# A list scheduler that reckons each GpSimd step of a 32x32 inverse longer: delta attention and two feed-forward stages on one core

## The chip, the core and the metric

The kernel runs on one core of a Trainium2 chip. The metric is the device time of one execution in microseconds; three runs of the kernel before were taken, and one execution was recorded by the hardware profiler. Engines: PE is TensorE (matrix products; PEld its weight loads), DVE is VectorE, ACT is ScalarE, POOL is GpSimd, SP is the queue that issues the DMAs.

## What is computed

Inputs are float32 (and are turned to float32 where they come as float64). Three stages follow each other:

```python
# attention: B=4, H=8, S=768, D=48, for each of 32 heads
k_n = k / (norm(k) + 1e-6)
for t in range(S):
    y[t] = q[t] @ state
    v_old = state.T @ k_n[t]
    state = state + beta[t] * outer(k_n[t], v[t] - v_old)
# first feed-forward, 3072 tokens, 384 -> 1024 -> 384
h = x @ w_in;  solu = h * softmax(h)
x = layernorm(solu) * g_ln @ w_out
# second feed-forward, 384 -> 2048 -> 384
out = relu(x @ w_in2) ** 2 @ w_out2
```

## The kernel before

**The work.** The recurrence is done in chunks of 64 tokens. Inside a chunk the sequential update is a triangular system, so each chunk needs the inverse of a unit lower triangular 64x64 matrix; it is built from inverses of 32x32 blocks. The 24 tiles (t = 0 to 23, each two chunks of four pairs of heads) are put in six groups of four (G0, `group`). For a tile, `e_tile` or its parts load q and k, form the products on PE (banks are read by ACT, which writes g, and DVE or POOL, which mask m), and store g in DRAM (gscr). When the four tiles of a group are there, `gammas` makes the factors from the norms and `inversion` (L835) inverts all 128 blocks of the group at once, one block to a partition: 30 columns, each a product (L910) and a sum (L927), columns from the tenth on in two parts. Then one product with gamma (L952) ends it. The result `it` is stored in DRAM (tscr); ACT copies it transposed to `ia` (L969), which is stored too (uscr). For each tile `load_tb` (L985) reads the blocks back as tbd and t2, `prep1` (L1062), `prep2` (L1078, needs t2) and `z` (L1105) apply the inverse on PE, and `a_mm` and `o_mm` run the recurrence. ACT copies the results: ys, tbd, zs (L1119).

The first group (g = 0) is inverted on DVE; the other five are inverted on GpSimd, one after the other. Inside an inverse the planner puts a small memset (L940) on GpSimd after every stretch of steps whose price passes 0.75 us. GpSimd also scales v by the norms (`load_kv`, L1042), does some masks and squares at the start, and makes the low halves `wgl` of the eight pieces of the first output weight (`load_w1o`, through `split`, L420). The weights come as 64-bit words: ACT (L458), DVE (L466 to L502) and ACT again (L539) decode them and scale them by g_ln, and ACT casts the high half wgh (L415).

The first feed-forward runs behind the attention, tile by tile (`moe1_front`: transposes L1204, products L1215, softmax and norm on DVE and ACT; `moe1_back`: transposes L1317, zh and zl), and its output product `moe1_out` (L1337, needs wgh and wgl) for each two tiles. The second feed-forward (L1480, L1524) starts when the attention's buffers are free. Products in float32 are split in a high and a low half and done as three matmuls.

**What sets the order.** The program is not written in the order in which it runs. Every operation is given to the class `Plan` (L116) with its engine, a price in us, the keys it reads and writes, and a priority (its due time). `Plan.order` (L159) runs a list scheduler forward over all operations: whenever an engine is free, it takes from the operations whose inputs are there the one with the smallest key. Between dependent operations it adds 0.1 us on GpSimd and ScalarE, 0.13 us on DVE, and 0.2 us between engines. For DMAs it reckons an issue time, a rate and a tail. Then it runs a backward pass, takes the ends of that as the new keys, and repeats this 12 times; the order of the round with the shortest reckoned span is what is emitted, as one in-order queue for each engine and one for the DMAs on SP. So a price affects nothing but the order. The price of one step on GpSimd is `c_pool` (L271), with n the elements of a partition:

```python
def c_pool(n, full=True):
    return 0.148 + n * (2.104e-3 if full else 1.667e-3)
```

In `inversion` every step goes through `one` (L864), which calls the local function `cost`; a product and the last step pass full=False. The mask `lower` (1.3 us) and the memsets (0.1 us) have prices of their own, and the counter `run`, which places the memsets, calls `c_pool` itself.

Of the kernel before, what the change touches and what calls it, by code (L numbers as in the profile page):

```python
# [262 lines left out]
def c_dve(n, fast=False):  # L263
    return 0.07 + n / (1920.0 if fast else 960.0)
# [6 lines left out]
def c_pool(n, full=True):  # L271

    return 0.148 + n * (2.104e-3 if full else 1.667e-3)
# [3 lines left out]
def tile_delta_moe_moe(  # L277
# [14 lines left out]
    v, act, pool, pe = nc.vector, nc.scalar, nc.gpsimd, nc.tensor  # L292
# [541 lines left out]

    def inversion(g, en, prio):  # L835

        eng, cost = (v, lambda n, full=True: c_dve(n) + 0.09) if en == "dve" else (pool, c_pool)
        gm = gm_[g % 2]
        it, itmp = it_[g % 2], junk[:, 512:] if g == 1 else itmp_
        kgm, kic, kia = ("A", "gm", g % 2), ("A", "itc", g % 2), ("A", "ia")  # L840
# [5 lines left out]
        n = 2 * (G0[g + 1] - G0[g])  # L846
# [54 lines left out]
        for j in range(1, HB - 1):  # L901
            nr = HB - 1 - j
            for q, (c0, c1) in enumerate(((0, min(j, s1)), (s1, j))):
                w_ = c1 - c0
                if w_ <= 0:
# [13 lines left out]
                    full=False,  # L919
# [35 lines left out]
            full=False,  # L955
# [197 lines left out]
    def o_mm(t):  # L1153
        first, last = t % NCH == 0, t % NCH == NCH - 1

        def mm():
            for i in range(2):
                for p in range(NP):
                    for h in range(2):
                        s = rows[h]  # L1160
                        if not last:
                            pe.matmul(ksp[heads[h], i, p], zs_[i][s, p, C:112], R[s, i, p], start=True, stop=True)
                        pe.matmul(  # L1163
                            xp[rows[1 - h], i, p],
                            zs_[i][s, p, 0:C],
                            R[s, i, p],
                            start=first and i == 0 and p == 0,
                            stop=True,
                            skip_group_check=True,
                        )  # L1170

        return mm, [("A", "zs", 0), ("A", "zs", 1), ("A", "r")], [("A", "a"), ("A", "o")]
# [393 lines left out]
    for t in range(T1):  # L1566
        wr = e_tile(t, -70 + t)
        norms(t, -62)
    gammas(0, -61)
    inversion(0, "dve", -55)  # L1570
    first_inv.append(plan.writer["A", "it", 0, 0])
    for t in range(T1, T2):
# [4 lines left out]

    gate.append(wr)
    inversion(1, "pool", PR["inv1"])
    load_w1i(0, 6, PR["w1i"])  # L1580
    for t in range(T2, LA):
# [16 lines left out]
    for t in range(NT + 3):  # L1598
        if t < NT:
            for g in range(2, NG):  # L1600
                if t == max(1, G0[g] - 5):
                    gammas(g, t + PR["inv"])
                    inversion(g, "pool", t + PR["inv"])
# [7 lines left out]
            parts, cost = [], 0.3  # L1611
# [23 lines left out]
            parts, cost = [o_mm(t)], 1.25  # L1635
# [113 lines left out]
```

## Time and profile before

| what | value |
|---|---|
| median of 3 runs | 900.76 us (897.88 to 901.03) |
| the profiled execution, own time | 896.73 us |
| its span, first to last instruction | 895.0 us |
| mean granted TensorE clock | 0.96 of full |
| busy: PE, PEld, DVE, ACT, POOL | 804.2, 748.0, 494.7, 449.6, 311.7 us |
| POOL idle from | 432 us on |

The page's first part gives busy times, its second the span in 40 slices, its fourth the chain of work that ended last, followed back from the end. The busy time of PE is modelled from pipelined matmuls. An idle time of an engine is put down to what released it; a group or a timeline row shows it in brackets ahead of the arrow. Times of the trace count from the start of the span.

### The profile page before, as it was taken

To read this page: it belongs to the slowest core of one execution; us is meant where nothing else is said; L and a number is where in the kernel's file an instruction comes from. 1 tells how busy PE (TensorE), PEld (TensorE's weight loads), DVE (VectorE), ACT (ScalarE), POOL (GpSimd) and SP (SyncE) were. 2 spreads that over 40 slices of the span, in tenths; PEclk is the share of its full clock that TensorE was granted. 3 is DMA by queue.
4 is the path that set the end of the run, shared out by engine and by line. 5 is a ranking of instruction groups with operands and counts; after the bars stand their busy time and mean duration, and the time that the engine had idled before them with its cause. 6 is when DMAs were issued, how large, how long until landed. Compare 5 with 4: busy or idle time off the path is not lost.

```text
span 895.0 us, 24146 instructions
## 1 busy us (share of the span) xinstructions
PE 804.2 (90%) x9904; PEld 748.0 (84%) x9904; DVE 494.7 (55%) x990; ACT 449.6 (50%) x996; POOL 311.7 (35%) x751
## 2 busy tenths in 40 slices
PE   5425759999978989999999999999999999999997
PEld 4324637888867878878889999999999999999997
DVE  5999765634974895775756444343334333343332
ACT  2315568675765675756666444343434333343333
POOL 5469989847978978920000000000000000000000
PEclk9975878999998999999999999999999999999999
DMA  9947866577687686466244311010101001010101
GB/s 243 275 119 175 251 160 172 138 158 187 176 254 190 198 204 188 145 178 182 88 130 127 112 48 53 1 54 1 53 1 38 17 1 53 1 27 1 27 1 27
DMA packets 139726, 99.71 MB, mean 111 GB/s; under 512 B 95072, under 2 KB 120672, under 8 KB 139616
## 3 DMA queue, kind: packets, MB, share of 16 engines
q1 hardware_dynamic: 139616, 98.18, 40.3%
q8 instruction: 77, 1.26, 0.6%
q14 instruction: 33, 0.27, 0.1%
HBM read 71.41 MB, written 26.74 MB: 110 GB/s over the span
## 4 chain that ended last, share of the span: by engine, by line
PE 63%; POOL 12%; DVE 7%; DMA 6%; ACT 5%; issue 3%; SPq 3%; ACTq 0%; POOLq 0%; DVEq 0%
PE acc L1524 22%; PE h L1480 22%; PE p_x L1337 7%; POOL it L927 6%; PE p_h L1215 5%; POOL junk L910 3%; SPq L300 3%; DMA raw<-in_w2i_dram 2%; POOL itmp L910 2%; PE p_tr L1317 2%; PE p_a L1132 1%; DMA m<-in_ktok_dram 1%; PE p_u L1105 1%; PE p_o L1163 1%; DVE zl L420 1%
## 5 line engine op out<-in xcount | busy, mean ns | idle before, releaser
L1501 DVE TENSOR_TENSOR xt<-xt 128x384 f32<-128x384 f32 x128 | 71.5, 558 | 167.3 <-ACT xt L1493 167.1
L1493 ACT ACTIVATE xt<-h 128x384 f32<-128x384 f32 x128 | 63.0, 492 | 167.1 <-PE h L1480 167.0
L1480 PE MATMUL h<-x1l,w2h 128*128 128x384 f32 x384 | 128.7, 335 | 0.0
L1480 PE MATMUL h<-x1h,w2h 128*128 128x384 f32 x384 | 128.6, 335 | 0.0
L1480 PE MATMUL h<-x1h,w2l 128*128 128x384 f32 x384 | 128.5, 335 | 0.0
L927 POOL TENSOR_TENSOR it<-it,itmp 128x72 f32<-128x72 f32 (+37 forms) x204 | 89.4, 454 | 4.6
L1524 PE MATMUL acc<-woh,xh 128*128 128x384 f32 x258 | 87.7, 340 | 0.7 <-ACT ot L1546 0.7
L1337 PE MATMUL p_x<-zh,wgh 128*128 128x256 f32 x288 | 86.2, 299 | 1.9 <-ACT xo L1351 1.8
L1524 PE MATMUL acc<-wol,xh 128*128 128x384 f32 x258 | 87.4, 339 | 0.0
L1524 PE MATMUL acc<-woh,xl 128*128 128x384 f32 x258 | 87.1, 338 | 0.0
L910 POOL TENSOR_TENSOR itmp<-it 128x72 f32<-128x72 f32 (+37 forms) x204 | 85.9, 436 | 2.2
L1337 PE MATMUL p_x<-zl,wgh 128*128 128x256 f32 x288 | 82.1, 285 | 0.0
L1337 PE MATMUL p_x<-zh,wgl 128*128 128x256 f32 x288 | 82.1, 285 | 0.0
L420 DVE TENSOR_TENSOR xl<-xt,xh 128x384 fp32r<-128x384 f32 x86 | 48.0, 558 | 44.7 <-ACT xh L415 44.4
L1480 PEld LDWEIGHTS h<-x1h,w2h 128*128 128x128 f32 x384 | 72.1, 188 | 0.0
L1480 PEld LDWEIGHTS h<-x1l,w2h 128*128 128x128 f32 x384 | 72.1, 188 | 0.0
L1480 PEld LDWEIGHTS h<-x1h,w2l 128*128 128x128 f32 x384 | 72.1, 188 | 0.0
L415 ACT CAST xh<-xt 128x384 fp32r<-128x384 f32 x86 | 44.1, 513 | 48.2 <-DVE xt L1501 47.0
L1215 PE MATMUL p_h<-w1h,xh 128*128 128x512 f32 x144 | 62.8, 436 | 3.3 <-DVE xl L420 3.3
L1337 PEld LDWEIGHTS p_x<-zh,wgh 128*128 128x128 f32 x288 | 55.2, 192 | 5.7 <-ACT xo L1351 2.9
L1215 PE MATMUL p_h<-w1l,xh 128*128 128x512 f32 x144 | 58.9, 409 | 0.0
L1215 PE MATMUL p_h<-w1h,xl 128*128 128x512 f32 x144 | 58.7, 408 | 0.0
(181 smaller groups left out, 1967.4 us busy)
## 6 DMA issues: line engine op xcount, KB each, us to landing
kql<-in_kin_dram SPq DMA_DIRECT2D x22, 512.0 KB, 6.5
kqe<-in_kin_dram SPq DMA_DIRECT2D x38, 192.0 KB, 6.5
raw<-in_w2i_dram SPq DMA_DIRECT2D x12, 512.0 KB, 5.2
raw<-in_w2o_dram SPq DMA_DIRECT2D x16, 384.0 KB, 4.2
gscr<-g SPq DMA_DIRECT2D x21, 256.0 KB, 4.2
m<-in_ktok_dram SPq DMA_DIRECT2D x24, 192.0 KB, 3.8
vt<-in_vtok_dram SPq DMA_DIRECT2D x24, 192.0 KB, 4.6
x1scr<-xo SPq DMA_DIRECT2D x12, 384.0 KB, 2.6
```

The source lines that it names most:

```text
L300: return add("sp", 0.06, lambda: nc.sync.dma_start(dst(), src()), r, w, prio, size, gate)
L415: add("act", c_act(n), lambda: act.copy(hi(), src()), r, [w[0]], prio)
L420: lambda: le.tensor_tensor(out=lo(), in0=src(), in1=hi().bitcast(F32), op=ALU.subtract),
L910: lambda tm=tm, j=j, nr=nr, w_=w_, c0=c0, c1=c1: eng.tensor_tensor(out=tm, in0=it[:, j + 1 :, j : j + 1].to_broadcast([P, nr, w_]), in1=it ...
L927: lambda tm=tm, j=j, c0=c0, c1=c1: eng.tensor_tensor(out=it[:, j + 1 :, c0:c1], in0=it[:, j + 1 :, c0:c1], in1=tm, op=ALU.add,),
L1215: pe.matmul(p_h[:, sl], xx[:, c], ww[:, c, sl], start=(c == 0 and k == 0), stop=(c == 2 and k == 2),)
L1317: pe.transpose(ptr[:, f], e[:, k * P : k * P + P], ident)
L1337: pe.matmul(p_x1[:, 0 : 2 * P], ww[:, f, c * P : c * P + P], zz[:, f], start=(f == 0 and k == 0), stop=(f == 7 and k == 2),)
L1480: pe.matmul(late["h2", ih], late[ww][:, c, s], xx[:, c], start=(c == 0 and k == 0), stop=(c == 2 and k == 2),)
L1493: lambda: act.activation(out=rt, in_=late["h2", ih], func=AF.Relu),
L1501: lambda: v.tensor_tensor(out=gg, in0=rt, in1=rt, op=ALU.mult),
L1524: pe.matmul(late["acc", a], gg[:, a * P : a * P + P], late[ww][:, f], start=(f == 0 and k == 0), stop=(f == 15 and k == 2),)
```

## The change

In `inversion` the price function is replaced. For DVE the price is as before, c_dve(n) + 0.09. For GpSimd each step is c_pool(n, full) + 0.12 us for g = 1, the second group, and c_pool(n, full) + 0.06 us for the groups behind it; before it was c_pool(n, full). Nothing else is edited.

```diff
     def inversion(g, en, prio):
 
-        eng, cost = (v, lambda n, full=True: c_dve(n) + 0.09) if en == "dve" else (pool, c_pool)
+        eng, slow = (v, 0.09) if en == "dve" else (pool, 0.12 if g == 1 else 0.06)
+        cost = lambda n, full: (c_dve(n) if en == "dve" else c_pool(n, full)) + slow
         gm = gm_[g % 2]
```

## Rows read from the trace of the kernel before

**Rows 1.** The page, part 4: shares of the chain that ended last, by engine.
```profile
PE 63%; POOL 12%; DVE 7%; DMA 6%; ACT 5%; issue 3%; SPq 3%; ACTq 0%; POOLq 0%; DVEq 0%
```

**Rows 2.** Stages: stretch, us, busy of PE, PEld, DVE, ACT, POOL; PEclk, DMA, GB/s.
```profile
100.00:124.00 24.00, 17.19 (x269) 13.12 (x267) 19.78 (x44) 11.20 (x28) 23.89 (x55) 0.79 0.58 153
124.00:145.00 21.00, 13.45 (x157) 9.65 (x157) 11.26 (x21) 17.83 (x37) 18.12 (x29) 0.67 0.77 203
145.00:178.00 33.00, 32.59 (x795) 28.64 (x796) 18.55 (x42) 24.10 (x60) 28.39 (x93) 1.00 0.58 160
360.00:387.00 27.00, 26.09 (x565) 22.84 (x554) 21.95 (x51) 19.69 (x45) 25.76 (x73) 1.00 0.55 161
```

**Rows 3.** Timeline of POOL, 52 to 139 us: start, us, instruction, idle before it.
```profile
52.11 2.34 POOL L891 TENSOR_TENSOR it<-it,gm 128x1024 f32<-128x1024 f32 x1 [16.38 <-DMA it<-gscr]
...
117.00 3.79 POOL L927 TENSOR_TENSOR it<-it,junk 128x40 f32<-128x40 f32 x2
...
121.79 1.91 POOL L952 TENSOR_TENSOR it<-it,gm 128x1024 f32<-128x1024 f32 x1
...
126.52 2.06 POOL L420 TENSOR_TENSOR wgl<-wst,wgh 128x384 fp32r<-128x384 f32 x2 [2.03 <-ACT wgh L415]
128.54 2.36 POOL L891 TENSOR_TENSOR it<-it,gm 128x1024 f32<-128x1024 f32 x1
...
137.49 1.33 POOL L420 TENSOR_TENSOR wgl<-wst,wgh 128x384 fp32r<-128x384 f32 x1
```

**Rows 4.** Timeline of ACT, 116 to 137 us.
```profile
123.74 1.93 ACT L969 COPY ia<-it 128x1024 f32<-128x1024 f32 x1 [6.84 <-POOL it L952]
125.48 0.56 ACT L1119 COPY zs<-p_u 128x448 f32<-128x448 f32 x1
...
135.78 0.52 ACT L415 CAST wgh<-wst 128x384 fp32r<-128x384 f32 x1
```

**Rows 5.** Waits, 100 to 146 us: who for whom, us in total, times, longest.
```profile
ACT ia L969 <- POOL it L952: 6.8, 1, 6.8
...
PE p_u L662 <- ACT zs L1119: 3.1, 1, 3.1
...
PE p_tr L1317 <- DVE zl L420: 2.6, 1, 2.6
...
POOL wgl L420 <- ACT wgh L415: 2.0, 1, 2.0
```

**Rows 6.** Busy POOL steps: second group (tile junk), and four later ones (itmp).
```profile
52.10:123.80 71.70, 59.15 (x102) 0.69 0.62 159
...
sum 234.00, POOL 172.16; mean POOL 43.04
```

**Rows 7.** Timeline of the DMA queue SP: stores of ia, loads of t2.
```profile
125.69 1.28 SPq L300 DMA_DIRECT2D uscr<-ia  x2
...
136.56 0.81 SPq L300 DMA_DIRECT2D t<-uscr  x2
```

**Rows 8.** DMA issues of the whole trace: count, KB each, median us to landing.
```profile
uscr<-ia SPq DMA_DIRECT2D x12, 128.0 KB, 6.2
t<-uscr SPq DMA_DIRECT2D x24, 64.0 KB, 2.0
```

**Rows 9.** Timeline of PE, 145 to 146 us: tile 4's second preparation.
```profile
145.07 0.45 PE L1078 MATMUL p_a<-ys,t 32*32 32x32 f32 x32
```

**Rows 10.** The chain that ended last, 236 to 300 us.
```profile
256.02 1.92 ACT ia L969
```

**Rows 11.** Stages of line L1337 alone: stretch, us, busy of PE, PEld.
```profile
124.00:145.00 21.00, 0.00 (x0) 0.00 (x0) 0.67 0.77 203
```

**Rows 12.** Timeline of DVE, 118 to 140 us: decode of first output weights.
```profile
118.53 1.01 DVE L492 SCALAR_TENSOR_TENSOR wst<-raw,wst 128x384 uint32<-128x384 uint32 x2
...
136.53 0.73 DVE L492 SCALAR_TENSOR_TENSOR wst<-raw,wst 128x384 uint32<-128x384 uint32 x1
...
137.87 1.37 DVE L502 SCALAR_TENSOR_TENSOR wst<-raw,wst 128x384 uint32<-128x384 uint32 x1
```

## The prediction, made before the changed kernel ran

> **What bounds the kernel now.** The page's chain gives TensorE most of the span and GpSimd a clear second place [rows 1]. The busy times by stage place the two: from 145 us on PE is busy nearly throughout at full granted clock, 32.59 of 33 us and later 26.09 of 27, while between 100 and 145 us it works 17.19 + 13.45 of 45 us, so 14.4 us idle, at a granted clock of 0.79 and 0.67, a mix of the 2.4 and 1.2 GHz levels [rows 2]. Whoever fills that hole with matrix work shortens the kernel; later there is little to fill. Next I ask what PE waits for there, and whether a wrongly reckoned GpSimd step stands behind it. GpSimd works on the second group's inverse from 52.11 to 123.70 us, 71.6 us long [rows 3]. ScalarE's copy ia<-it (L969) needs its result. ScalarE came to that copy at 123.74 - 6.84 = 116.90 us and stood still until 123.74, and behind it in its in-order queue stood zs, the casts wgh and the next weight's work [rows 4]. The table of waits shows who was held up in turn: PE 3.1 us for zs, 2.6 us for zl, which DVE makes from ScalarE's zh, and GpSimd 2.0 us for wgh [rows 5]. So the copy stands too early in ScalarE's order, because the planner believes that the inverse ends sooner than it does.
>
> **What the change does.** It removes and adds no instruction. Each inverse on GpSimd has 51 products, 51 sums and three single steps priced through the changed function: 105 steps. The second group is reckoned 105 x 0.12 = 12.6 us longer, each of the four later ones 105 x 0.06 = 6.3 us. The lower mask (1.3 us) and the 30 small memsets keep their price and their places, since their counter does not use the new term; DVE's first inverse keeps its 0.09. What changes is the order of each engine's queue and the DMA queue's, which are computed from these prices.
>
> How good is the new price? The 102 steps are reckoned at 0.148 each plus elements x 0.001667 or 0.002104, which sums to 33.8 us; with the change 46.0 us (second group) and 39.9 us (later groups). The trace has 59.15 us for the second group and 43.04 us in the mean of the other four [rows 6]. So both prices move towards the truth and neither passes it. With the 0.1 us that the planner allows between dependent steps, and the other operations, I work out 50.6 us for an undisturbed inverse before, 63.2 us and 56.9 us after, against 71.6 us and windows of 58.5 us in the mean, both with some foreign work and waits in them.
>
> **Term 1, the hole on ScalarE.** The copy moves back by up to 12.6 us of ScalarE's work. What then stands ahead of it (zs, two wgh casts, and the decode and transposed halves after them) can run in the 6.84 us. The price on PE is what it waited through this hold: 3.1 + 2.6 = 5.7 us [rows 5]. Upper bound: all of PE's idle time there, 14.4 us [rows 2]. Lower bound: 2.0 us, if GpSimd's own wait for wgh is all that goes. I take 5.7 us, the nearest rows to the mechanism. It stays gained at the end only because PE has matrix work without holes right behind it [rows 2]. A fuller PE would also spend less of the stretch at 1.2 GHz; I count nothing for that, it lies inside the upper bound.
>
> **Term 2, the copy comes too late.** If ScalarE has no other hole, it now reaches ia at 116.90 + 12.6 = 129.5 us, 5.8 us after the inverse. Queued behind the copy is tile 4's way: 1.93 us copy, 1.28 us to issue the two stores, 6.2 us to land, 0.4 us to issue the load (0.81 for two) and 2.0 to land it [rows 4, 7, 8], so t2 is there at 129.5 + 11.8 = 141.3 us. PE's matmul that needs it ran at 145.07 [rows 9]. Today's cover is 3.8 us; if everything else moves up by 5.7 us, tile 4 is 1.9 us late. I cost it at nothing, because PE then has the products L1337 to do; without that cover the gain shrinks to 3.8 us.
>
> **Term 3, later groups.** ia of the fourth group is on the chain at 256.02 [rows 10], and PE is full around the later ends [rows 2]. I cost the four shifts of 6.3 us at 0: the new reckoning is nearer the windows. Bounds: a gain of 0.9 us, all of PE's idle time around the last of them (27 - 26.09) [rows 2], and a loss of 5.7 us if one boundary falls as empty as the second group's is now.
>
> **Sum.** The profiled execution took 896.73 us (span 895.0, 1.7 us around it): 896.73 - 5.7 = 891.0. The median of the runs stands 4.0 us above that execution, so I put the forecast at 900.76 - 5.7 = **895.0 us**. A measurement can tell about 0.5%, 4.5 us, from no change; the forecast lies just past it.
>
> **Rivals.** *A, the whole hole goes.* The casts wgh and their subtractions on GpSimd come early, the first products L1337 move ahead of tile 4, and PE idles no more before 145 us: -14.4 us, 886.4 us. For: no product L1337 runs between 124 and 145 us [rows 11], though PE has the time. Against: DVE decodes the last weights only at 136 to 139 us [rows 12]. Chance 0.08.
>
> *B, the gain is given back.* If GpSimd's inverses set the pace of the later tiles, only their start counts. The third group's inverse starts at 128.54 after two subtractions that waited 2.03 us for wgh [rows 3]; that wait is all that can go: 898.7 us, no measurable change. For: ia at 256.02 is on the chain [rows 10]. Against: PE at 97 to 99% [rows 2]. Chance 0.14.
>
> *C, GpSimd is held inside the second inverse (slower).* Between two dependent steps the planner lets any ready work in. Of the eight subtractions wgl the third and fourth ran 2.8 us behind the inverse's end, the sixth at 137.49 [rows 3]; with an end reckoned 12.6 us later more of them come in ahead of it. In the true run GpSimd would then wait in order for ScalarE's casts, the sixth of which ended at 136.30 [rows 4]. With these four let in and the casts no earlier, the inverse ends no sooner than 136.3 + 1.3 (the subtraction) + 1.9 (its last step, L952) = 139.5 us; 11.8 us on, at 151.3, t2 lands that was used at 145.07: +6.2 us, 907.0 us. It decides against the change when the inverse ends after 145.07 + 4.5 - 11.8 = 137.8 us. For: the rule of the queue above. Against: with ScalarE free at 116.9 the casts come earlier too. Chance 0.25, the share of mixed shifts with it.
>
> *D, DVE and GpSimd collide.* The second inverse's steps are long where DVE combines two tiles from SBUF: two sums of 40 elements took 3.79 us at 117.0 [rows 3], while DVE ran L492 [rows 12]. If work released early on ScalarE brings the decode of the last two weights into the inverse, their L492 and L502 (0.73 + 1.37 us for one weight) [rows 12] hold GpSimd up to 4.2 us longer: 900.76 - 5.7 + 4.2 = 899.3 us, no measurable change. Chance 0.08.
> The Trainium skill, page SBUF — State Buffer, section Who interferes with whom, says that a VectorE instruction with two SBUF inputs and a GpSimd instruction that reads SBUF block each other for the whole instruction; the 3.79 us beside DVE's L492 agree. By that rule no fixed price per step can be right, for the excess follows DVE's order, which the change itself moves.
>
> That the order does not change at all I leave out: 525 prices change, and every queue is computed from them.
>
> **How the numbers follow.** The forecast's mechanism has 0.45, of which 0.37 is past 4.5 us and 0.08 short of it. Faster: 0.37 + 0.08 (A) = 0.45. Same: 0.08 + 0.14 + 0.08 = 0.30. Slower: 0.25. The range goes from A's 886.4 to C's 907.0, widened by 1.6 us, half of what the three runs of before lie apart (897.88 to 901.03): 885 to 909. What lies outside, above all a heavier C, I give 2 in 10.
>
> **What would show it.** Right: ScalarE's wait for the inverse at L969 falls from 6.8 us to under 1 us; zs and wgh stand ahead of the copy in its queue; PE's idle between 100 and 145 us falls from 14.4 to about 9 us; L1337 starts before 145; the count of instructions is unchanged. Wrong: the second inverse ends after 130 us with more L420 inside it (C), sums of few elements take microseconds at other places (D), or the stage before 145 is shorter and PE's idle time after it longer by as much (B).

## The result and the profile after

The changed kernel took 910.77 us (median of four runs, 903.19 to 912.69) where the kernel before, run in turn with it, took 899.56 us: a ratio of 1.0128 with a 95% interval of 1.0095 to 1.0160. It is slower by 1.3%, where 895.0 us were forecast. A second measurement, below, gave 1.0149. The profiled execution shown here is the shortest of the four: 903.19 us, span 901.5 us. Lines behind the edit are one higher than before (L969 is L970, L1078 is L1079, L1337 is L1338).

The page's chain by engine, which answers to [rows 1], and the stages of [rows 2]:

```profile
PE 69%; DVE 8%; ACT 6%; POOL 6%; DMA 5%; issue 3%; SPq 2%; ACTq 0%; DVEq 0%; POOLq 0%
```

```profile
100.00:124.00 24.00, 15.45 (x245) 12.23 (x246) 21.92 (x42) 14.21 (x35) 21.52 (x43) 0.72 0.69 183
124.00:145.00 21.00, 12.96 (x91) 10.61 (x90) 11.01 (x19) 14.53 (x25) 12.67 (x36) 0.88 0.36 110
145.00:178.00 33.00, 30.93 (x737) 26.77 (x737) 10.76 (x23) 18.92 (x52) 26.98 (x84) 0.87 0.59 148
```

PE's idle time between 100 and 145 us did not fall from 14.4 to 9 us: it is 45 - 15.45 - 12.96 = 16.6 us. And the stage behind it, which was full at full clock, now has 2.1 us of idle time and a granted clock of 0.87.

GpSimd's timeline through the second inverse, to be held against [rows 3]:

```profile
115.32 2.38 POOL L892 TENSOR_TENSOR it<-it,gm 128x1024 f32<-128x1024 f32 x1 [2.48 <-ACT gm L819]
...
129.10 1.92 POOL L953 TENSOR_TENSOR it<-it,gm 128x1024 f32<-128x1024 f32 x1
...
145.99 1.00 POOL L420 TENSOR_TENSOR wgl<-wst,wgh 128x384 fp32r<-128x384 f32 x1 [9.22 <-ACT wgh L415]
```

The third group's first product (L892) stands inside the second inverse, after a wait of 2.48 us for its factors, and so do its mask, its first steps and three wgl (98.5 to 104.5 us). The second inverse ends at 129.10 + 1.92 = 131.0 us, 7.3 us later than before, though its 102 steps are busy for no more than before (57.50 us against 59.15 [rows 6]). Then GpSimd stands 9.22 us for a cast.

ScalarE's timeline, to be held against [rows 4], and the DMA queue's against [rows 7]:

```profile
136.80 0.59 ACT L415 CAST zh<-p_tr 128x512 fp32r<-128x512 f32 x1 [4.00 <-PE p_tr L1318]
...
139.83 1.92 ACT L970 COPY ia<-it 128x1024 f32<-128x1024 f32 x1
...
145.41 0.51 ACT L415 CAST wgh<-wst 128x384 fp32r<-128x384 f32 x1
```

```profile
131.05 0.34 SPq L300 DMA_DIRECT2D tscr<-it  x1
141.77 1.29 SPq L300 DMA_DIRECT2D uscr<-ia  x2
143.18 2.83 SPq L300 DMA_DIRECT2D tbd<-tscr  x5
```

The wait of 6.84 us at the copy is gone, as forecast. But the copy now runs 8.8 us after the inverse's end, behind a wait of 4.00 us for PE. And the queue SP, which works in order, holds tile 4's loads tbd<-tscr behind the two stores of ia: their source was stored at 131.05, and they are issued at 143.18. The chain that ended last shows it in one piece (start, us, what):

```profile
139.93 1.82 ACT ia L970
141.75 0.34 ACT wst L458
142.09 0.27 SPq L300
...
143.18 2.81 DMA tbd<-tscr
...
146.13 0.83 PE p_a L1063 x32
```

PE's timeline there, with the row that answers to [rows 9] last but one:

```profile
143.17 1.11 PE L1318 MATMUL p_tr<-ident,ez 128*128 128x128 f32 x4 [4.98 <-ACT ez L1259]
...
144.93 0.41 PE L1338 MATMUL p_x<-zh,wgl 128*128 128x256 f32 x1
...
146.13 0.83 PE L1063 MATMUL p_a<-tbd,g 32*32 32x32 f32 x32 [0.57 <-DMA tbd<-tscr]
...
153.22 0.53 PE L1079 MATMUL p_a<-ys,t 32*32 32x32 f32 x32
...
154.02 0.28 PE L1338 MATMUL p_x<-zl,wgh 128*128 128x256 f32 x1
```

Tile 4's second preparation comes at 153.22 where it came at 145.07. PE waits 4.98 us for ez (the exponentials of the first feed-forward), which ScalarE makes only behind the late copy; after that wait its products take 0.41 us each and, from 153.9 on, 0.28 us: the lower and the higher of the clock's two levels (granted clock 0.52 from 143.1 to 153.7 us and 1.00 from there to 160). The first product L1338 ran at 136.5 us (145.4 before). So the hole was not filled; it opened again at the copy. Twelve of the products that should have covered tile 4 ran before the hole; the rest stand in PE's queue behind the transposes that need ez.

### The profile page after: what moved, and what is told of

It reads as the page before. It is cut to its first block, busy times and chain, and to the rows that moved or that the text cites. A ratio compares the mean times of both kernels' runs of the same rounds, so it can differ in the third digit from the quotient of the medians.

```text
span 901.5 us, 24161 instructions
## 1 busy us (share of the span) xinstructions
PE 801.2 (89%) x9904; PEld 746.3 (83%) x9904; DVE 497.3 (55%) x990; ACT 450.3 (50%) x996; POOL 306.0 (34%) x751
## 4 chain that ended last, share of the span: by engine, by line
PE 69%; DVE 8%; ACT 6%; POOL 6%; DMA 5%; issue 3%; SPq 2%; ACTq 0%; DVEq 0%; POOLq 0%
PE acc L1525 22%; PE h L1481 22%; PE p_h L1216 9%; PE p_x L1338 8%; POOL it L928 2%; POOL junk L911 2%; SPq L300 2%; DMA raw<-in_w1i_dram 1%; DMA m<-in_ktok_dram 1%; PE p_tr L1318 1%; PE p_u L1106 1%; DVE wst L492 1%; PE p_a L1133 1%; DVE sc L1231 1%; ACT ez L1259 1%
## 5 line engine op out<-in xcount | busy, mean ns | idle before, releaser
L1338 PE MATMUL p_x<-zh,wgh 128*128 128x256 f32 x288 | 87.6, 304 | 6.5 <-ACT xo L1352 6.4
L928 POOL TENSOR_TENSOR it<-it,itmp 128x72 f32<-128x72 f32 (+37 forms) x204 | 87.1, 442 | 4.0
L1338 PE MATMUL p_x<-zh,wgl 128*128 128x256 f32 x288 | 82.9, 288 | 0.0
L1338 PE MATMUL p_x<-zl,wgh 128*128 128x256 f32 x288 | 82.8, 287 | 0.0
L1338 PEld LDWEIGHTS p_x<-zh,wgh 128*128 128x128 f32 x288 | 56.0, 194 | 10.4 <-ACT xo L1352 7.7
## 6 DMA issues: line engine op xcount, KB each, us to landing
gscr<-g SPq DMA_DIRECT2D x21, 256.0 KB, 6.7
```

Source lines behind the costliest of these rows:

```text
L928: lambda tm=tm, j=j, c0=c0, c1=c1: eng.tensor_tensor(out=it[:, j + 1 :, c0:c1], in0=it[:, j + 1 :, c0:c1], in1=tm, op=ALU.add,),
L1338: pe.matmul(p_x1[:, 0 : 2 * P], ww[:, f, c * P : c * P + P], zz[:, f], start=(f == 0 and k == 0), stop=(f == 7 and k == 2),)
```

## The experiments

Ratios are to runs of before on the same chip, with the 95% interval. Inverse ends and copy times are from each kernel's one profiled execution. The diffs show the lines that make the edit, some drawn together; the bookkeeping around them is left out.

**Which group's price.** e1 keeps the second group's 0.12, e2 the later groups' 0.06, e3 puts 0.002 on all of them.

```diff
-        eng, slow = (v, 0.09) if en == "dve" else (pool, 0.12 if g == 1 else 0.06)
+        eng, slow = (v, 0.09) if en == "dve" else (pool, 0.12 if g == 1 else 0.0)   # e1
+        eng, slow = (v, 0.09) if en == "dve" else (pool, 0.0 if g == 1 else 0.06)   # e2
+        eng, slow = (v, 0.09) if en == "dve" else (pool, 0.002)                     # e3
```

> The 0.12 us stay on the second group, the 0.06 us on the later ones are taken away. Theory H (the loss comes from the second group's inverse: reckoned so long that other work is let in and the copy ia on ScalarE comes after it is needed): as slow as the change, 906 to 914 us, and ScalarE's copy of the second group starts several us after that inverse's end. Theory L (the later groups' 0.06 us do it): back to the kernel before, 897 to 902 us. Theory S (any shift of prices reshuffles the order, and the tuned order is lost): somewhere in 900 to 915 us, with no sign from which part was kept.

> The 0.06 us stay on the later groups, the second group's 0.12 us are taken away. Theory H: as the kernel before, 897 to 903 us, with ScalarE again standing at the second group's copy. Theory L: as slow as the change, 906 to 914 us. Theory S: 900 to 915 us, slower than before by over 0.5%.

> Every GpSimd step is reckoned 0.002 us longer, a hundredth of the change and of no meaning as a price. Theory H and theory L: as the kernel before within 0.5%, 896 to 904 us. Theory S: the order of the queues changes as a whole and the time moves by over 0.5%, most likely to the slow side, 904 to 912 us.

Measured: e1 906.75 us, 1.0102 (1.0068 to 1.0137); e2 898.66, 1.0012 (0.9984 to 1.0041); e3 897.61, 0.9994 (0.9972 to 1.0016). The second group's price alone makes a loss of this size; the later groups' price does nothing that can be measured; and that an order is computed anew costs nothing by itself. In e1 seven wgl stand inside the second inverse, which ended at 138.0 us, and its copy ran at 141.2 us. GpSimd waits for two of their casts (waits of e1, 51 to 138 us):

```profile
POOL wgl L420 <- ACT wgh L415: 4.2, 2, 2.6
```

In e3 the second inverse ended at 119.2 us, 4.5 us sooner than before, and nothing was gained by it.

**One inverse after the other.** e4 lets no step of a later inverse in before the last one's end.

```diff
             [*kraws, kgm],
             [*kts, kic],
+            last_inv if g > 1 else (),
         )
```

> The change as it is, but the inverses of the third to sixth group may not begin before the one ahead of them has ended, so the third group's work cannot stand inside the second group's inverse. Theory H: the second inverse ends by 124 us instead of 131 and part of the loss comes back, 900 to 906 us. Theory S: 900 to 915 us, no matter where the second inverse ends. Theory L: no better than the change, 908 to 914 us.

Measured: 913.57 us, 1.0169 (1.0134 to 1.0204). With the third group's steps shut out, all eight wgl came into the second inverse instead, and it ended at 133.8 us. So the mixing of two inverses isn't needed for the loss; the planner fills the believed spare time with something either way.

**Does the end of an inverse set the time?** e5, e6 and e12 leave the order of before untouched and put six more masks on the tile `it` near the end of the second, the third or the sixth inverse (g = 1, 2, 5).

```diff
+        def diagonal():
+            for _ in range(6 if g == 1 else 0):
+                pool.affine_select(out=it, in_=it, pattern=[[1, HB], [-1, HB]], base=0,
+                    channel_multiplier=0, compare_op=ALU.is_gt, fill=0.0)
+            eng.memset(it.rearrange("p r s -> p (r s)")[:, 0 :: HB + 1], 1.0)
...
-            lambda: eng.memset(it.rearrange("p r s -> p (r s)")[:, 0 :: HB + 1], 1.0),
+            diagonal,
```

> The kernel before, with the same order on every engine; only the mask of the second group's inverse is applied six more times at its end (it changes nothing in the numbers and is not in the planner's prices), so that this inverse ends some 7.7 us later. Theory P (the inverses pace the kernel: second inverse, tiles 4 and 5, their products for tiles 14 and 15, fourth inverse, tiles 12 and 13, sixth inverse, last tiles): slower by 5 to 9 us, 903 to 907 us, and the fourth and sixth inverse end later by as much. Theory B (PE is the bound from 145 us on, and fills what is late with other work): slower by 0 to 2 us, 897 to 900 us.

> As the run before this one, but the six extra masks stand at the end of the third group's inverse, which is followed by 12.7 us in which GpSimd waits. Theory P in the form of that loop: no more than 0 to 3 us, 897 to 901 us, because the third inverse is not on it. Theory Q (it is the plain sum of GpSimd's work that paces): slower by 6 to 8 us, 904 to 906 us. Theory B: 897 to 900 us.

> The kernel before with its order; six more masks, 7.7 us, at the end of the sixth (last) group's inverse. Theory P: its end paces the last four tiles, slower by 5 to 8 us, 903 to 906 us. Theory B (PE has enough other work): 0 to 2 us slower, 898 to 900 us.

Measured: e5 905.51 us, 1.0098 (1.0060 to 1.0136); e6 901.28, 1.0038 (1.0006 to 1.0069); e12 907.01, 1.0096 (1.0067 to 1.0125). The masks took 7.93 us. GpSimd's timelines: of e5 the second inverse's last step (L965), the fourth's first product (L891), the fourth's and the sixth's last step; of e6 the last steps of the fourth and sixth.

```profile
129.28 1.91 POOL L965 TENSOR_TENSOR it<-it,gm 128x1024 f32<-128x1024 f32 x1
...
205.62 2.36 POOL L891 TENSOR_TENSOR it<-it,gm 128x1024 f32<-128x1024 f32 x1 [6.16 <-ACT gm L819]
262.09 1.91 POOL L965 TENSOR_TENSOR it<-it,gm 128x1024 f32<-128x1024 f32 x1
...
392.67 1.92 POOL L965 TENSOR_TENSOR it<-it,gm 128x1024 f32<-128x1024 f32 x1
```

```profile
256.58 1.92 POOL L965 TENSOR_TENSOR it<-it,gm 128x1024 f32<-128x1024 f32 x1
...
383.47 1.92 POOL L965 TENSOR_TENSOR it<-it,gm 128x1024 f32<-128x1024 f32 x1
```

In e5 the 7.5 us of the second inverse (131.2 against 123.7) are there at the fourth's end (264.0 against 256.0), at the sixth's (394.6 against 385.5) and at the end. Where they reach PE is in the waits, of e5 (118 to 146 us), of e12 (378 to 412) and of e6 (178 to 215):

```profile
ACT ia L982 <- POOL it L965: 15.3, 1, 15.3
...
PE p_u L662 <- ACT zs L1132: 10.8, 1, 10.8
```

```profile
ACT ia L982 <- POOL it L965: 12.2, 1, 12.2
...
PE p_x L1350 <- ACT xo L1364: 9.2, 1, 9.2
```

```profile
ACT ia L982 <- POOL it L965: 5.4, 1, 5.4
...
PE p_x L1350 <- ACT xo L1364: 3.3, 1, 3.3
```

ScalarE comes to its copy ia in time and stands there until the held inverse ends: 15.3 us in e5 (6.8 before [rows 5]), 12.2 us in e12 (3.7 before) and 5.4 us in e6 (not at all before, where this copy ran 1.8 us behind its inverse's end). Next in ScalarE's queue is zs in e5 and xo, the copy of p_x, in the other two, and PE waits for just that: 7.7, 8.2 and 3.3 us longer than before. The medians rose by 7.4 (905.51 - 898.09), 10.2 and 3.2 us. So in an order where ScalarE stands at the copy, the delay goes to PE at once through ScalarE's queue, and in e5 and e12 it isn't made up later. (The profiled execution of e6, 895.56 us, shows no loss; its median does.)

A longer way is possible beside it. The fourth inverse's first product waits for gm: its factors need tiles 14 and 15, whose key products come in the steps of tiles 4 and 5 (LA = 10). That would make a loop: second inverse, tiles 4 and 5, fourth inverse, tiles 12 and 13, sixth inverse, the last four tiles. That this loop sets the pace is not shown: PE's wait at the copy is enough for the loss, and in e6 the fourth inverse ends 2.5 us late while the sixth ends on time.

**The weights behind the second inverse.** e7 puts the subtractions wgl, in the changed kernel, behind the second inverse's end (with e4's edit); e8 does so in before.

```diff
             prio if lo_eng == "dve" else prio - 40,
+            after=() if lo_eng == "dve" else last_inv,
         )
```

> The change with its prices, but the eight subtractions wgl may not run on GpSimd before the second group's inverse has ended, and the later inverses run one after the other. Theory P with the weights' subtractions as the cause: the second inverse ends by 124 us instead of 131, and the time comes back to 897 to 903 us. Theory S (the order as a whole is lost): it stays at 906 to 914 us although the second inverse ends early.

> The kernel before with its prices, and the eight subtractions wgl behind the end of the second group's inverse (two of them stand inside it in the kernel before, 2 us). Theory P: the second inverse ends 2 to 4 us earlier and the kernel gains up to that, 894 to 898 us. Theory B and theory S: 896 to 902 us.

Measured: e7 901.57 us, 1.0059 (1.0034 to 1.0084), with the second inverse's end at 122.3 and its copy at 126.8 us; against e4, from which it differs by this edit alone, 12 us less. e8: 898.33, 1.0015 (0.9994 to 1.0035), with the end at 117.1 us. Keeping foreign work out of the second inverse gives more than half of that loss back, but an end sooner than before's brings nothing.

**The same order, one place moved.** For the rest the changed kernel's order was taken as planned and single operations moved in one engine's queue, the program then being written out in an order that keeps every queue and every dependence. e9: the copy ia of the second group five places up in ScalarE's queue. e10: wgl and the third group's steps behind the second inverse's end in GpSimd's queue. e11: both.

```diff
+        act_q = queues["act"]                          # e9, e11
+        k = act_q.index(inv_copy[1])
+        act_q.insert(k - 5, act_q.pop(k))
+        q = queues["pool"]                             # e10, e11
+        a, b = q.index(inv_ops[1][0]), q.index(inv_ops[1][-1])
+        away = {*wgl_ops, *inv_ops[2]}
+        mid = q[a : b + 1]
+        q[a : b + 1] = [i for i in mid if i not in away] + [i for i in mid if i in away]
```

> The changed kernel with its order; only ScalarE's copy ia of the second group is moved five places up in ScalarE's queue, ahead of two casts zh, two squares and one exponential, to where ScalarE stood when the inverse ended. Theory P, with the late copy as a part of the loss: tile 4's first products (L1063), held behind the stores of ia in the DMA queue, move from 146 to 138 to 141 us, and the kernel takes 903 to 908 us. Theory P without it (only the end of the inverse counts): as the change, 908 to 912 us.

> The changed kernel with its order; only on GpSimd the three subtractions wgl and the steps of the third group's inverse that stand inside the second group's inverse are moved behind its end. Theory P: the second inverse ends at 119 to 123 us instead of 131. If the copy on ScalarE still comes at 138 to 140 us, most of the loss stays, 905 to 911 us; if the end of the inverse counts, 899 to 904 us. Theory S: no change, 908 to 913 us.

> Both moves of the two runs before this one together. Theory P: the second inverse ends at 119 to 123 us, the copy follows within some 5 us, tile 4's first products come by 138 us, and the kernel takes 897 to 902 us, as the kernel before. Theory S: 906 to 913 us, since all other queues keep the changed order.

Measured: e9 902.59 us, 1.0055 (1.0030 to 1.0081); e10 920.03, 1.0233 (1.0188 to 1.0277); e11 913.76, 1.0181 (1.0118 to 1.0244). e9's copy ran at 132.90 us and tile 4's loads were issued from 136.36 on; still, PE came to its products only at 146.93, with these rows before them (timeline of PE, e9):

```profile
144.60 1.11 PE L1328 MATMUL p_tr<-ident,ez 128*128 128x128 f32 x4 [3.26 <-ACT ez L1269]
...
146.93 0.65 PE L1073 MATMUL p_a<-tbd,g 32*32 32x32 f32 x32
```

In e10 the second inverse ended at 121.2 us, and yet all came later, for the buffers wst are freed by wgl (waits, 118 to 170 us):

```profile
POOL wgl L422 <- ACT wgh L417: 14.7, 1, 14.7
ACT wst L462 <- POOL wgl L422: 14.6, 1, 14.6
```

ScalarE waits for a subtraction that GpSimd has not come to, and the copy ia behind it runs at 152.2 us. In e11 it waits 13.8 us there, and the copy, five places up, still runs at 140.6 us, 19.8 us behind its inverse's end (120.7); so the 897 to 902 us expected of both moves are missed. An early end of the inverse is worth nothing when the copy stands behind something else.

**Again, and tile 4 first.** e13 is the changed kernel once more. e14 takes e9 and moves, on PE, tile 4's two preparations and tile 3's state products ahead of the last transposes and 18 products p_x, and on ScalarE their copies with them.

```diff
+        act_q.insert(act_q.index(prep[4, 1] + 1) - 7, act_q.pop(act_q.index(prep[4, 1] + 1)))
+        k = act_q.index(prep[4, 2] + 1)
+        act_q[k - 3 : k + 4] = act_q[k : k + 4] + act_q[k - 3 : k]
+        q = queues["pe"]
+        up = [prep[4, 1], a_op[3], prep[4, 2]]
+        b = q.index(up[2])
+        a = q.index(up[0]) - 2
+        q[a : b + 1] = up + [i for i in q[a : b + 1] if i not in up]
```

> The changed kernel itself, on the same chip and beside the same runs of before as the next kernel, since its first four runs spread from 903 to 913 us. Tile 4 theory: the loss is there on any chip, 905 to 912 us against 898 of before, with tile 4's first products near 146 us. Chance theory (the four runs were a bad draw): within 0.5% of before, under 902.5 us.

> The changed kernel's order, with tile 4's way alone moved up: the copy ia five places in ScalarE's queue, and on PE tile 4's first products, tile 3's state products and tile 4's second products ahead of the last transposes p_tr and 18 products p_x (with ScalarE's ys seven and its four tbd copies three places up). The second inverse keeps its late end near 132 us. Tile 4 theory: the second products come at 145 to 147 us as in before instead of 153, so most of the loss is gone: 897 to 902 us, and its last inverse ends at 386 to 391 us. Inverse theory (the late end of the inverse, and with it the third group's inverse behind it on GpSimd, is the loss, whatever tile 4 does): 903 to 907 us as with the copy alone, last inverse near 394. PE theory (PE's total work bounds after 145 us; what is moved back costs as much as what is moved up): also 903 to 907 us, but with PE's work no nearer to before at 178 us.

Measured: e13 911.03 us, 1.0149 (1.0115 to 1.0182); e14 904.51, 1.0079 (1.0055 to 1.0103), beside the same runs of before. Tile 4's second preparation is back at its place of before:

```profile
144.02 0.57 PE L1089 MATMUL p_a<-ys,t 32*32 32x32 f32 x32 [1.53 <-DVE r L1159]
```

The second inverse still ended at 131.3 us. So the late copy, with tile 4's way behind it, is about half of the loss (14.0 us fall to 7.5), and what was expected by the tile 4 theory (897 to 902) is missed. e9, with this preparation still at 153.90 us, gave as much as e14; the two can't be told apart, so these runs show that the copy matters, with what stands behind it; that PE's place for tile 4 does too they don't show.

**The other waits.** e15: the eighth wgl, for which GpSimd waits 9 to 11 us, 24 places later in its queue. e16: e14 and e15 together. e17: the fifth inverse's first steps, which stand among the fourth's last ones and wait there for gm, behind the fourth's end. e18: all three.

```diff
+        q = queues["pool"]                             # e15, e16, e18
+        k = max(q.index(i) for i in wgl_ops)
+        q.insert(k + 24, q.pop(k))
+        a, b = q.index(inv_ops[4][0]), q.index(inv_ops[3][-1])   # e17, e18
+        away, mid = set(inv_ops[4]), q[a : b + 1]
+        q[a : b + 1] = [i for i in mid if i not in away] + [i for i in mid if i in away]
```

> The changed kernel's order with one instruction moved: the eighth subtraction wgl, for which GpSimd waits 9.2 us inside the third group's inverse, stands 24 places later in GpSimd's queue. Hold theory (half of the loss goes through this wait: the third inverse ends 15 us late, runs into the fourth, and that ends 12 us late): third inverse ends near 191, fourth near 259, and the time falls by 4 to 8 us to 903 to 907. Tile 4 theory (only tile 4's place counts; the third group's end had 12.7 us to spare): the time stays at 909 to 912.

> The edits of the last two kernels together: tile 4's way moved up and the eighth wgl moved back. Both holds theory: what is left of the loss goes, third inverse near 190, fourth near 256, sixth near 387, 896 to 900 us, no more than 0.4% from before. If the third inverse's late end is not what the first kernel with tile 4 moved up still loses, it stays at 903 to 906 us.

> The changed kernel's order with the steps of the fifth group's inverse that stand among the last steps of the fourth's moved behind the fourth's end on GpSimd, nothing else. There GpSimd waits 3.9 to 4.7 us for the fifth group's gammas and then runs the fifth's first product and mask (2.4 and 1.7 us), with the fourth's last steps queued behind. Held-inverse theory (this hold lies on the way of tiles 12 and 13): the fourth inverse ends 7 to 9 us sooner, near 262, and the time falls by 3 to 7 us, to 904 to 908. If the hold is absorbed before the sixth inverse: the fourth ends as much sooner, and the time stays at 908 to 912.

> Tile 4's way moved up, the eighth wgl moved back, and the fifth group's head behind the fourth's end. If tile 4's place and this hold are the change's two losses: the fourth inverse ends at 256 to 259, the sixth at 384 to 388, 895 to 900 us, within 0.3% of before. If the remaining 0.65% lies elsewhere: 901 to 904 us.

Measured: e15 907.87 us, 1.0101 (1.0076 to 1.0127), not clearly below e13; e16 903.69, 1.0065 (1.0041 to 1.0088); e17 910.15, 1.0163 (1.0130 to 1.0196); e18 902.38, 1.0086 (1.0052 to 1.0120). None of the three moves adds anything measurable to e14, or to e9. GpSimd's waits from 131 to 205 us, e13 and then e15:

```profile
POOL wgl L420 <- ACT wgh L415: 10.6, 1, 10.6
POOL vt L1043 <- DMA vt<-in_vtok_dram: 8.6, 3, 4.6
POOL vt L1043 <- DMA m<-in_ktok_dram: 5.2, 1, 5.2
```

```profile
POOL vt L1053 <- DMA vt<-in_vtok_dram: 19.2, 3, 10.7
POOL vt L1053 <- DMA m<-in_ktok_dram: 3.7, 1, 3.7
POOL wgl L422 <- ACT wgh L417: 0.7, 1, 0.7
```

The wait for the cast is gone, and GpSimd waits as long for the next tile's v: 24.4 us and 23.6 us in all. In e17 the fourth inverse ended 11.7 us sooner than in e13 (259.4 against 271.1), and its copy ran no sooner (timelines of GpSimd and of ScalarE, e17):

```profile
257.45 1.91 POOL L961 TENSOR_TENSOR it<-it,gm 128x1024 f32<-128x1024 f32 x1
```

```profile
272.03 2.14 ACT L980 COPY ia<-it 128x1024 f32<-128x1024 f32 x1
```

This is the second inverse's case once more: the copy's place in ScalarE's queue keeps the time, not the inverse's end.

The start of the second, fourth and sixth group's copies ia, and each kernel's own profiled execution (us):

| kernel | 2nd | 4th | 6th | execution |
|---|---|---|---|---|
| before | 123.7 | 256.0 | 385.5 | 896.7 |
| e3, 0.002 on all | 119.2 | 255.0 | 387.8 | 899.2 |
| e2, later groups' price | 121.0 | 256.7 | 392.9 | 898.8 |
| e6, third held | 123.7 | 258.5 | 385.4 | 895.6 |
| e5, second held | 131.2 | 264.0 | 394.6 | 905.1 |
| e12, sixth held | 123.6 | 254.9 | 394.8 | 906.8 |
| e9, copy moved up | 132.9 | 269.5 | 400.0 | 905.1 |
| e18, all three moved | 131.9 | 266.1 | 396.9 | 902.2 |
| the change, shown above | 139.8 | 268.1 | 397.1 | 903.2 |
| e13, the change again | 143.3 | 271.3 | 401.9 | 912.2 |
| e10, inverse alone | 152.2 | 281.0 | 410.5 | 915.6 |

From the sixth copy to the end there are 505 to 512 us in each row, and 505 to 513 us in the nine kernels left out, so the end follows that copy within 8 us. That is no finer than half of the loss: e2's sixth copy comes 7.4 us later than before's, and it loses nothing, so the copies are a guide to the time and not its whole account.

## Why the prediction was wrong

**Term 1, the hole on ScalarE:** half right. ScalarE no longer waits at the copy, the work behind it ran before it, and the products L1338 started at 136.5 us instead of 145.4. That PE pays for ScalarE's standing at the copy, e5 and e12 bear out. But PE's idle time up to 145 us grew from 14.4 to 16.6 us: the 5.7 us were taken back by new waits, 4.98 us for ScalarE's ez the longest. The gain assumed that the hole closes; it moved to the copy's new place.

**Term 2, the copy comes too late: the step that failed.** The mechanism was named and both its size and its cover were wrong. Size: I put the copy at 129.5 us and tile 4 at 1.9 us late; the copy ran at 139.83 (143.29 in e13) and tile 4's second preparation 8.1 us late. Three things were left out: the inverse itself ended 7.3 us later; ScalarE had other holes on the way (4.00 us for PE); and SP holds tile 4's loads tbd behind the stores of ia, which I counted for t2 alone. Cover: "I cost it at nothing, because PE then has the products L1337 to do" took it that only tile 4 stands behind the copy. But ez does too, PE waited 4.98 us for it, and most of those products stand behind that wait. In place of nothing, the copy's place cost over half of the loss: five places up, with no other move, the ratio falls from 1.0149 (e13) to 1.0055 (e9), about 8 us. By which of the things behind the copy (ez, the stores, the loads) stays open: in e9 PE still waits 3.26 us for ez. For tile 4 alone the cover may have held: in e14 its second preparation runs 9.9 us sooner than in e9, and the time is no shorter.

**Term 3, later groups:** its 0 holds for the price alone (e2, 1.0012). But "PE is full around the later ends" was read from two stretches, and the bound of 0.9 us from one that ends at 387 us. Behind the fourth's end PE was not full (stage of before):

```profile
256.00:300.00 44.00, 37.24 (x609) 32.50 (x610) 26.15 (x43) 27.55 (x63) 35.94 (x86) 0.88 0.75 213
```

And a stage that is full in before is not so when its inverse is late: in e12 PE waited 9.2 us for what ScalarE had behind the sixth copy.

**Rivals.** C came nearest: foreign work inside the second inverse, and a wait for the casts. In the changed kernel the inverse ended at 131.0 us, short of the 137.8 us from which I let it decide, and the long wait for wgh lay behind the end, where moving it changed nothing (e15); there the loss came through the copy instead. In e1, with the same price for the second group, it is nearly C as written: seven wgl inside, 4.2 us of waits for wgh, an end at 138.0 us, and 906.75 us where C had 907.0. B's premise, that the inverses set the pace of the later tiles, is left open: e5 and e12 fit it, but PE's wait behind the copy is enough for what they lost. I gave it 0.14 and took it to mean no loss. A didn't come. D isn't shown: the second inverse's steps were busy for 1.7 us less than before, not more.

**Not settled.** e1 isolates the price, e5 shows that a late second inverse suffices for a loss of this size in an order where ScalarE stands at the copy, and e9 that the copy's place is over half of the change's loss, in which ScalarE does not stand there. With tile 4's way restored, 0.65 to 0.86% is left (e14, e16, e18). In e18 the copy of the fourth group runs 12.7 us behind the end of its inverse (266.1 against 253.4) and that of the sixth 4.2 us (396.9 against 392.7); that these are the rest was only argued, for moving them up wasn't tried. No version beat the kernel before.

## What to carry to other kernels

A high busy share of an engine in the stage before does not show that it covers what comes late: hold one suspected link by a known time in an unchanged order, see whether the delay is still there at the end, and read in that run's waits where the busy engine took it up, before a longer chain is blamed. When a scheduler's price goes up, look for the instruction that consumes the priced result on each other in-order queue, because it is placed by the believed end and everything queued behind it, DMA issues too, moves with it. And a truer price of one step need not make a better order: the changed price is nearer to the measured steps [rows 6], and its order is 1.3% slower. Nor is an earlier end worth anything by itself: e3, e8 and the kernel before had the second inverse end between 117 and 124 us and took the same time.

## What the runs showed that was not expected

In before two sums of 40 elements took 3.79 us [rows 3]; in e5, with the same order, the two products just ahead of such sums took that long, and the sums did not. GpSimd's timeline of e5, the products and the sums, and DVE's beside it:

```profile
115.48 4.28 POOL L910 TENSOR_TENSOR junk<-it 128x40 f32<-128x40 f32 x2
119.72 0.44 POOL L927 TENSOR_TENSOR it<-it,junk 128x40 f32<-128x40 f32 x2
```

```profile
115.86 0.54 DVE L1193 TENSOR_TENSOR s<-s,p_a 112x384 f32<-112x384 f32 x1
...
117.73 1.02 DVE L492 SCALAR_TENSOR_TENSOR wst<-raw,wst 128x384 uint32<-128x384 uint32 x2
118.66 1.02 DVE L502 SCALAR_TENSOR_TENSOR wst<-raw,wst 128x384 uint32<-128x384 uint32 x2
```

The products end 0.08 us after DVE's unbroken run of decodes (118.66 + 1.02 = 119.68), and the sums of the same size take a tenth of their time. In both runs the long steps lie beside DVE's work on the weights, so the same step is short or long by where it falls, and a fixed price per step is a mean at best. That DVE is what holds them fits these rows; no run took DVE's work away.

The other thing is a queue that holds data back while there is little traffic: between 131.39 and 141.77 us SP issues nothing, with loads behind the stores of ia whose data had been stored at 131.05, and the DMA share of that stage is 0.36 after 0.77 before [rows 2]. A low DMA share there was the sign of a hold, not of spare room.
